# Float64 decode by masks on VectorE, block diagonals by a multiply, and a planner that knows partition turns: one fused attention, expert and mixing kernel on one core

## The chip, the cores and the metric

One core of a Trainium2 chip runs the whole program. The metric is device microseconds of one execution, from first to last instruction with a small fixed part around it. Engines are named as the profile names them: PE is TensorE (PEld its weight loads), DVE is VectorE, ACT is ScalarE, POOL is GpSimd, SP issues the DMAs. Each engine works through its own queue in order and waits on semaphores that the others raise.

## The reference, cut to what matters

Three stages follow one another for each of 8 batches of 576 tokens. In the reference's words, cut:

```python
k_p = k.reshape(B, H, 72, 8, D).mean(axis=3)          # pooled keys, 8 heads of 64
v_p = v.reshape(B, H, 72, 8, D).mean(axis=3)
x = softmax(q @ k_p.T / 8) @ v_p                      # attention, heads joined to 512
# 4 experts: causal attention with 64-wide heads, top 2 of 4 gates
out += gate_e * (softmax_causal(x @ wq[e], x @ wk[e]) @ (x @ wv[e]) @ wo[e])
theta = out @ w_theta
y = w_tok_r @ (out * cos(theta)) + w_tok_i @ (out * sin(theta))
u = out + y
result = u + maximum(u @ w_ch, 0)
```

Three of the weights, `w_theta`, `w_tok` and `w_ch`, come to the kernel as 64-bit floats. They have to be turned into pairs of 32-bit numbers (a rounded high part and the remainder) before PE can use them.

## The kernel before

Every product is made of three matmuls on a high and a low part (`mm3`), and the parts are made by ACT (a copy that rounds, the high part) and DVE or POOL (a subtraction, the low part). A first stage, up to about 500 us, runs attention and the experts for the 8 batches; a second stage mixes tokens and channels for the 8 batches.

The program is written as a list of operations, each with its engine, and a planner (`Plan`) issues them. `Plan.add` records an operation and its dependencies, `price` gives it an assumed cost, `arrange` gives it a due time from two tables (`PARTS` for the part of the program, `SHIFT` for engine and tile), and `issue` simulates the five queues and picks, one at a time, the operation that can start first, ties by due time. The result is a fixed order for each engine. So a change of costs or tables moves instructions everywhere, though none is added by it.

The parts that the change touches:

- `pool_kv` (L713 to L752): for each batch it sums groups of 8 keys and values by three `tensor_tensor` adds (on POOL; some on DVE for batch 0, by `FIRST_DVE`), tiles `kt1`, `vt1` and `vt2`. Two heads lie in the two halves of the 128 partitions and go to a block-diagonal operand: `kbd` by two ACT copies of 64 partitions each, `vbd` by two ACT copies and two subtractions of 64 partitions each. The other two blocks hold zeros that were written once at the start by POOL. The rest of the values goes to `vrh`, `vrl` (64 wide) and is spread by two multiplications with a mask `hm` to `vrb0` and `vrb1`.
- `attn_half` (L754): per tile of 128 queries, scores go to PSUM `s`, DVE takes the maximum `mx`, ACT takes the exponentials `pp`: eight activations with an accumulated sum, or, for tiles named in `WHOLE` (batch 0: tiles 1 to 4; later batches: tile 0), two DVE additions, one activation over all 576 columns and one DVE sum `l`. Then `pm` and `pq` are scaled, turned by PE (`t`) and split to `pa` and `pr`. The low part of `pr` lies in its upper 64 partitions.
- `decode` (L672): a task of 256 or 288 columns. DMA brings `d_raw`; ACT adds 768 to the high words as floats (`d_s`) and takes the sign; DVE shifts and joins the words in `d_raw`; ACT takes the absolute value; POOL multiplies `d_s`; ACT copies to `d_hi`; POOL subtracts to `d_lo`; two DMAs take the parts to DRAM (`thD`, `tokD`). 26 tasks run among the first stage, 8 more (`wch`, straight to `chs`) at the start of the second.
- `load` (L538): the DMAs `kraw`, `qraw`, `vraw`, `vrem` on SP's queue.

## Time and profile before

| what | value |
| --- | --- |
| median of 3 runs | 982.76 us (980.51 to 984.83) |
| the profiled execution, its time | 980.56 us |
| its span, first to last instruction | 978.8 us |
| PE busy | 916.0 us, 94% of the span |
| ACT busy | 650.3 us, 66% |
| DVE busy | 600.0 us, 61% |
| POOL busy | 516.7 us, 53% |
| mean granted TensorE clock | 0.992 of full speed |

Busy time is the time in which an engine had at least one instruction in flight. Instructions of one engine overlap at their ends, so sums of durations are above busy time. The profile gives stretches of the span (windows), groups of instructions by tile and shape (lines), what ended an engine's waits, the chain of work that ended last, and the instructions in order of time.

### The profile page before, as it was taken

To read this page: it belongs to the slowest core of one execution; us is meant where nothing else is said; L and a number is where in the kernel's file an instruction comes from. 1 tells how busy PE (TensorE), PEld (TensorE's weight loads), DVE (VectorE), ACT (ScalarE), POOL (GpSimd) and SP (SyncE) were. 2 spreads that over 40 slices of the span, in tenths; PEclk is the share of its full clock that TensorE was granted. 3 is DMA by queue.
4 is the path that set the end of the run, shared out by engine and by line. 5 is a ranking of instruction groups with operands and counts; after the bars stand their busy time and mean duration, and the time that the engine had idled before them with its cause. 6 is when DMAs were issued, how large, how long until landed. Compare 5 with 4: busy or idle time off the path is not lost.

```text
span 978.8 us, 19095 instructions
## 1 busy us (share of the span) xinstructions
PE 916.0 (94%) x6384; PEld 858.5 (88%) x6384; DVE 600.0 (61%) x1718; ACT 650.3 (66%) x2026; POOL 516.7 (53%) x693
## 2 busy tenths in 40 slices
PE   2888999999899999999888999999999999999998
PEld 2887988898889899988866799999999999999998
DVE  5877887787878788887756745272424534262412
ACT  4689989798888999987768864262535444363510
POOL 7877777577386755544355774261625335151420
PEclk9999999999999999999989999999999999999999
DMA  9444445335444433334277413020110202010001
GB/s 279 138 143 122 122 123 150 115 108 140 119 118 116 136 96 87 89 103 115 51 232 243 154 44 92 1 85 13 38 56 13 80 1 70 1 38 13 25 25 49
DMA packets 78434, 91.63 MB, mean 94 GB/s; under 512 B 11264, under 2 KB 60928, under 8 KB 78336
## 3 DMA queue, kind: packets, MB, share of 16 engines
q1 hardware_dynamic: 78336, 90.41, 31.4%
q8 instruction: 51, 0.84, 0.4%
q14 instruction: 47, 0.39, 0.1%
HBM read 58.34 MB, written 26.28 MB: 86 GB/s over the span
## 4 chain that ended last, share of the span: by engine, by line
PE 64%; ACT 17%; DVE 8%; DMA 4%; POOL 3%; issue 3%; SPq 1%; POOLq 0%; ACTq 0%; DVEq 0%
PE acc L466 46%; PE s L466 14%; PE t L466 4%; ACT pp L466 4%; ACT pt L466 2%; DMA kh<-kh 2%; ACT pev L466 2%; ACT qs L466 1%; DVE s L466 1%; ACT kh L466 1%; ACT pa L466 1%; DVE pa L466 1%; DMA qraw<-in_qT_dram 1%; ACT xT L466 1%; DVE kl L466 1%
## 5 line engine op out<-in xcount | busy, mean ns | idle before, releaser
L466 PE MATMUL acc<-toks,z 128*128 128x288 f32 x1536 | 242.3, 297 | 2.0 <-ACT z L466 1.0
L466 PEld LDWEIGHTS acc<-toks,z 128*128 128x128 f32 x1536 | 223.9, 188 | 9.5 <-POOL z L466 1.8
L466 POOL TENSOR_TENSOR us<-u,us 128x288 fp32r<-128x288 f32 x64 | 51.9, 811 | 198.4 <-ACT us L466 198.3
L466 PE MATMUL acc<-xT,wqs 128*128 128x256 f32 (+1 forms) x768 | 123.3, 303 | 3.4 <-DVE logit L466 1.4
L466 PE MATMUL acc<-us,chs 128*128 128x288 f32 x768 | 114.1, 297 | 0.6 <-DVE o L466 0.5
L466 PEld LDWEIGHTS acc<-xT,wqs 128*128 128x128 f32 x768 | 106.4, 189 | 7.5 <-PE acc L466 3.4
L466 PEld LDWEIGHTS acc<-us,chs 128*128 128x128 f32 x768 | 107.9, 188 | 5.0 <-DVE o L466 1.5
L466 DVE TENSOR_TENSOR u<-acc,xt 128x288 f32<-128x288 f32 x64 | 29.1, 455 | 132.4 <-PE acc L466 132.4
L466 ACT CAST us<-u 128x288 fp32r<-128x288 f32 x64 | 27.6, 431 | 120.6 <-DVE u L466 120.5
L466 POOL TENSOR_TENSOR z<-zf,z 128x512 fp32r<-128x512 f32 x64 | 81.9, 1298 | 33.7 <-ACT z L466 33.6
L466 POOL TENSOR_SCALAR pev<-pev,lb,G 128x128 f32<-128x128 f32 (+4 forms) x80 | 52.5, 657 | 72.6 <-DVE lb L466 30.0
L466 DVE TENSOR_TENSOR pt<-t,pt 128x512 fp32r<-128x512 f32 (+4 forms) x160 | 75.7, 484 | 15.2 <-ACT pt L466 13.2
L466 ACT ACTIVATE pp<-s,mx 128x72 f32<-128x72 f32 x232 | 74.6, 336 | 6.6 <-DVE mx L466 6.0
L466 PE MATMUL acc<-wvs,xT 128*128 128x260 f32 x480 | 77.6, 292 | 1.2 <-DVE kl L466 0.4
L466 DVE CUSTOM_DVE_ANT_0 s<-s,mask 128x128 f32<-128x128 f32 (+2 forms) x144 | 69.6, 494 | 14.7 <-PE s L466 12.7
L466 ACT CAST pt<-t 128x512 fp32r<-128x512 f32 (+4 forms) x160 | 67.8, 437 | 13.8 <-PE t L466 12.9
L466 PE MATMUL s<-kbd,qraw 128*128 128x144 f32 x320 | 60.3, 311 | 16.2 <-DMA qraw<-in_qT_dram 12.3
L466 PE MATMUL acc<-pt,v 128*128 128x320 f32 (+4 forms) x416 | 68.1, 296 | 5.6 <-ACT yg L466 1.6
L466 PE MATMUL s<-kh,qs 128*128 128x128 f32 (+2 forms) x192 | 62.3, 355 | 10.3 <-DMA kh<-kh 8.0
L466 PEld LDWEIGHTS acc<-pt,v 128*128 128x128 f32 x416 | 60.7, 191 | 11.2 <-ACT yg L466 3.1
L466 PEld LDWEIGHTS acc<-wvs,xT 128*128 128x128 f32 x480 | 65.5, 189 | 4.0 <-ACT yg L466 0.8
L466 PE MATMUL s<-wos,ys 128*128 128x512 f32 x192 | 66.1, 402 | 0.4 <-DVE zf L466 0.3
(177 smaller groups left out, 2244.8 us busy)
## 6 DMA issues: line engine op xcount, KB each, us to landing
qraw<-in_qT_dram SPq DMA_DIRECT2D x40, 256.0 KB, 3.6
out_dram<-o SPq DMA_DIRECT2D x64, 144.0 KB, 1.8
kraw<-in_kT_dram SPq DMA_DIRECT2D x15, 576.0 KB, 4.1
yraw<-ygD SPq DMA_DIRECT2D x16, 512.0 KB, 4.3
vraw<-in_vm_dram SPq DMA_DIRECT2D x15, 512.0 KB, 4.1
d_raw<-in_wtok_dram SPq DMA_DIRECT2D x18, 288.0 KB, 2.9
...
```

The lines of the kernel that those rows point to most:

```text
L466: o.ins = o.fn(*[a.real() if isinstance(a, View) else a for a in o.args], **{k: a.real() if isinstance(a, View) else a for k, a in o.kw.it ...
```

## The change

1. Decode. Two of ACT's passes (add and sign) become one DVE `tensor_scalar` that yields 0 or 1 for a word that is to be flushed; the absolute value becomes a mask in DVE's shift and one more DVE `scalar_tensor_tensor` that puts the sign and top bit back. ACT keeps the rounding copy, POOL its two operations. The pair goes to one tile `d_both` and by one DMA to DRAM.
2. Block diagonals. `kbd` and the doubled values are made by one multiplication with a column mask (`half`, `half64`) over 128 partitions, on POOL (DVE for some of batch 0); ACT rounds `vbd` by one copy and POOL subtracts once. All the sums share one tile `kv`. `vrh` and `vrl` become the two halves of one tile, with one multiplication by `hm`; `pq` is written twice so that `pr` has two whole tiles. Zero fills at the start go.
3. `WHOLE` for later batches is now tiles 0 and 2.
4. The planner adds 118 ns when an operation's first partitions differ from those of the one before on its engine (`TURN`), assumes a longer DMA (`DMA_LAT` 1700, and 1.7 times the bytes between on-chip tiles), and has new tables with a few parts of their own for the last batch of the first stage and the first of the second.

```diff
-WHOLE = {1, 2, 3, 4}, {0}
+WHOLE = {1, 2, 3, 4}, {0, 2}
-    "first": (-1302.83, 63.19), "kv first": (-249.24, 366.9), "attn first 0": (-2208.92, 30.55),
+    "first": (467.48, 10.11), "kv first": (72.08, 204.57), "attn first 0": (-1468.16, 177.1),
...
+        if eng == "DMA" and all(isinstance(a, View) and not a.root.pool.dram for a in args[:2]):
+            o.bytes *= 1.7
+    TURN = 118.0
+
-    DMA_ISSUE, DMA_LAT, DMA_RATE, DMA_ALL, DMA_SLOT, RELEASE = 600.0, 1300.0, 184.0, 262.0, 150.0, 130.0
+    DMA_ISSUE, DMA_LAT, DMA_RATE, DMA_ALL, DMA_SLOT, RELEASE = 600.0, 1700.0, 184.0, 262.0, 150.0, 130.0
...
-                t = free[e]
                 for o in cs:
+                    t = free[e] + (self.TURN if o.base != base[e] else 0.0)
...
-        A.activation(s, hi_w.bitcast(F32), AF.Copy, bias=FLUSH)
-        V.tensor_scalar(t, hi_w, 3, 0x40000000, op0=OP.logical_shift_left, op1=OP.bitwise_xor)
+        V.tensor_scalar(s, hi_w.bitcast(F32), FLUSH, FLUSH, op0=OP.add, op1=OP.not_equal)
+        V.tensor_scalar(t, hi_w, 3, 0x3FFFFFFF, op0=OP.logical_shift_left, op1=OP.bitwise_and)
         V.scalar_tensor_tensor(t, lo_w, 29, t, op0=OP.logical_shift_right, op1=OP.bitwise_or)
-        A.activation(s, s, AF.Sign, bias=flush)
-        A.activation(t.bitcast(F32), t.bitcast(F32), AF.Abs)
+        V.scalar_tensor_tensor(t, hi_w, -0x40000000, t, op0=OP.bitwise_and, op1=OP.bitwise_or)
         P.tensor_tensor(s, s, t.bitcast(F32), op=OP.mult)
         A.copy(hi, s)
         P.tensor_tensor(lo, s, f(hi), op=OP.subtract)
...
-        parts = decode(src, n, dec)
-        for d, p in zip(dst, parts):
-            D.dma_start(d, f(p))
+        D.dma_start(dst, f(decode(src, n, dec)))
...
-            for e in range(2):
-                s_ = slice(64 * e, 64 * e + 64)
-                A.activation(kbd[s_, p:p + n, e], t[s_, :, 0], AF.Copy, scale=1.0 / 64)
+            X.tensor_tensor(kbd[:, p:p + n], t[:, :, 0:1].to_broadcast([128, n, 2, 72]),
+                            half64[:, None, :, None].to_broadcast([128, n, 2, 72]), op=OP.mult)
...
-            for e in range(2):
-                s_ = slice(64 * e, 64 * e + 64)
-                A.copy(vbd[0][s_, p:p + n, e], t[s_, :, 0])
-                X.tensor_tensor(vbd[1][s_, p:p + n, e], t[s_, :, 0], f(vbd[0][s_, p:p + n, e]), op=OP.subtract)
+            X.tensor_tensor(t[:, :, 2:4], t[:, :, 0:1].to_broadcast([128, n, 2, 64]),
+                            half[:, None, :, None].to_broadcast([128, n, 2, 64]), op=OP.mult)
+            A.copy(vbd[0][:, p:p + n], t[:, :, 2:4])
+            X.tensor_tensor(vbd[1][:, p:p + n], t[:, :, 2:4], f(vbd[0][:, p:p + n]), op=OP.subtract)
...
-            X.tensor_tensor(pq[:, 0], pp[:, :, 64:72], l[:, :, None].to_broadcast([128, 8, 8]), op=OP.mult)
+            X.tensor_tensor(pq, pp[:, None, :, 64:72].to_broadcast([128, 2, 8, 8]),
+                            l[:, None, :, None].to_broadcast([128, 2, 8, 8]), op=OP.mult)
...
-            A.copy(pr[0:64, o:o + new], t1[:64, 0, n_])
-            V.tensor_tensor(pr[64:128, o:o + new], t1[:64, 0, n_], f(pr[0:64, o:o + new]), op=OP.subtract)
+            A.copy(pr[0][:, o:o + new], t1[:, 0, n_])
+            V.tensor_tensor(pr[1][:, o:o + new], t1[:, 0, n_], f(pr[0][:, o:o + new]), op=OP.subtract)
```

Three places in the issue order show it. First, SP's queue from the start of the program, before:

```order
L466 DMA vraw<-in_vm_dram 128x1024
L466 DMA kraw<-in_kT_dram 128x1152
L466 DMA pm<-in_vm_dram 128x512
L466 DMA vrem<-in_vr_dram 64x512
L466 DMA pev_161<-in_kT_dram 128x576
L466 DMA pev_164<-in_kT_dram 128x576
L466 DMA pm<-in_vm_dram 128x512
L466 DMA qraw<-in_qT_dram 128x4x128 x3
```

and now (`pev` holds keys here, `pm` values, `pod` a weight):

```order
L486 DMA kraw<-in_kT_dram 128x1152
L486 DMA pev_95<-in_kT_dram 128x576
L486 DMA pev_107<-in_kT_dram 128x576
L486 DMA vrem<-in_vr_dram 64x512
L486 DMA pm<-in_vm_dram 128x512 x2
L486 DMA qraw<-in_qT_dram 128x4x128
L486 DMA pod_177<-in_wvg_dram 128x260
L486 DMA vraw<-in_vm_dram 128x1024
```

The keys now come first, one query tile is asked for before the large `vraw`, and the other two query tiles come later.

Second, ACT's queue behind its first activation, before:

```order
L466 CAST vbd_95<-vt_175 64x2x64 x2
L466 ACTIVATE kbd<-kt_191 64x2x72 x2
L466 CAST vrh<-vt_205 64x64
L466 ACTIVATE kbd<-kt_213 64x72 x2
L466 CAST vrh<-vt_205 64x64
L466 ACTIVATE pp_150,suma_138<-s,mx 128x72 x4
```

and now:

```order
L486 CAST wvs_211<-pod_177 128x260
L486 ACTIVATE pp_157,suma_145<-s,mx 128x72 x8
L486 CAST wvs_211<-pod_183 128x260
L486 CAST vbd_249<-kv 128x256
L486 CAST wvs_211<-pev_95 128x260
```

ACT no longer stands between the sums and `kbd`; the eight exponentials of the first tile follow a weight's rounding directly.

Third, DVE's queue around the first 288-wide decode task, before:

```order
L466 RECIPROCAL l<-l 128x8
L466 TENSOR_SCALAR d_raw<-d_raw 128x288
L466 SCALAR_TENSOR_TENSOR qs_166<-acc,qs_166 64x320
L466 TENSOR_TENSOR pr<-t,pr 64x128
L466 TENSOR_TENSOR pa_3326<-t,pa_3317 128x4x128
```

and now (the task's two `scalar_tensor_tensor` follow some twenty rows on):

```order
L486 TENSOR_REDUCE m_1743<-gates_164 128x5
L486 TENSOR_SCALAR d_s<-d_raw 128x288
L486 TENSOR_REDUCE lb<-sum_132 128x2
L486 RECIPROCAL m_1743<-m_1743 128x5
L486 TENSOR_SCALAR d_t<-d_raw 128x288
L486 RECIPROCAL lb<-lb 128x2
```

DVE has two instructions of the first kind where it had one.

## Rows read from the trace of the kernel before

**Rows 1.** Windows: stretch; its length; PE, PEld, DVE, ACT, POOL busy; PEclk; DMA share; GB/s.

```profile
100.00:480.00 380.00, 359.17 (x2630) 336.04 (x2630) 306.01 (x1063) 336.06 (x1275) 235.82 (x373) 1.00 0.40 112
480.00:560.00 80.00, 69.55 (x388) 57.81 (x387) 53.82 (x123) 63.91 (x148) 45.20 (x44) 0.96 0.63 196
560.00:979.00 419.00, 415.19 (x2889) 398.13 (x2887) 167.48 (x292) 180.40 (x337) 158.95 (x144) 1.00 0.12 38
```

**Rows 2.** The page's chain that ended last, share of the span by engine.

```profile
PE 64%; ACT 17%; DVE 8%; DMA 4%; POOL 3%; issue 3%; SPq 1%; POOLq 0%; ACTq 0%; DVEq 0%
```

**Rows 3.** DVE's waits, 100 to 480 us: total us, times, longest us.

```profile
DVE xT L466 <- ACT xT L466: 8.7, 16, 2.5
...
DVE kl L466 <- ACT kh L466: 5.4, 8, 1.0
```

**Rows 4.** Groups on ACT by shape, 100 to 480 us: busy us, mean ns | idle before.

```profile
L466 ACT ACTIVATE pp<-s,mx 128x72 f32<-128x72 f32 x184 | 59.3, 338 | 2.3 <-DVE mx L466 1.9
...
L466 ACT ACTIVATE d_s<-d_s,flush 128x288 f32<-128x288 f32 x18 | 9.8, 546 | 0.2
L466 ACT ACTIVATE d_raw<-d_raw 128x288 f32<-128x288 f32 x18 | 8.6, 480 | 1.5 <-DVE d_raw L466 1.4
L466 ACT ACTIVATE d_s<-d_raw 128x288 f32<-128x288 f32 x18 | 8.6, 479 | 1.8 <-DMA d_raw<-in_wtok_dram 1.3 <-POOL d_lo L466 0.4
...
L466 ACT ACTIVATE kbd<-kt 64x144 f32<-64x144 f32 x20 | 6.5, 324 | 0.6 <-PE s L466 0.3
...
L466 ACT ACTIVATE pp<-pp 128x576 f32<-128x576 f32 x5 | 3.4, 684 | 2.1 <-DVE pp L466 2.1
```

**Rows 5.** ACT in order of time, from 14 us: start us, length us.

```profile
14.42 0.31 ACT L466 ACTIVATE pp<-s,mx 128x72 f32<-128x72 f32 x1
...
14.72 0.32 ACT L466 ACTIVATE pp<-s,mx 128x72 f32<-128x72 f32 x1
```

**Rows 6.** Groups on DVE by shape, 100 to 480 us, columns as in rows 4.

```profile
L466 DVE SCALAR_TENSOR_TENSOR d_raw<-d_raw 128x288 int32<-128x288 int32 x18 | 8.5, 472 | 0.3
...
L466 DVE TENSOR_SCALAR d_raw<-d_raw 128x288 int32<-128x288 int32 x18 | 5.7, 319 | 0.3 <-ACT d_s L466 0.2
...
L466 DVE TENSOR_TENSOR pp<-s,mx 128x288 f32<-128x288 f32 x10 | 4.4, 454 | 0.1
...
L466 DVE TENSOR_REDUCE l<-pp 128x8 f32<-128x584 f32 x5 | 3.8, 756 | 1.0 <-ACT pp L466 1.0
```

**Rows 7.** DVE in order of time, from 252 us, columns as in rows 5.

```profile
252.15 0.47 DVE L466 CUSTOM_DVE_ANT_0 s<-s,mask 128x256 f32<-128x256 f32 x1
...
252.53 0.48 DVE L466 TENSOR_TENSOR kl<-acc,kh 64x320 fp32r<-64x320 f32 x1
253.09 0.16 DVE L466 TENSOR_REDUCE lb<-sum 128x2 f32<-128x4 f32 x1
```

**Rows 8.** Groups on POOL by shape, 100 to 480 us, columns as in rows 4.

```profile
L466 POOL TENSOR_TENSOR pm<-pp,l 128x512 f32<-128x512 f32 x29 | 30.7, 1058 | 24.0 <-ACT pev L466 5.4 <-DVE l L466 5.2 <-ACT d_raw L466 3.9
...
L466 POOL TENSOR_TENSOR kt<-kt 128x288 f32<-128x288 f32 x9 | 7.3, 811 | 0.1
```

**Rows 9.** All engines in order of time, first 20 us: start, length, idle before and its releaser.

```profile
12.28 1.78 PE L466 MATMUL s<-kbd,qraw 128*128 128x144 f32 x6 [12.28 <-DMA qraw<-in_qT_dram]
...
16.46 0.53 ACT L466 ACTIVATE kbd<-kt 64x72 f32<-64x72 f32 x2
...
17.05 2.77 PE L466 MATMUL s<-kbd,qraw 128*128 128x144 f32 x10 [2.99 <-ACT kbd L466]
```

**Rows 10.** Instructions of tile d_raw over the whole span: min/median/max ns.

```profile
L466 DVE TENSOR_SCALAR d_raw<-d_raw x34: 254/310/2429, 43.2 to 588.4; 128x288 int32<-128x288 int32 x18, 128x256 int32<-128x256 int32 x16
```

**Rows 11.** POOL and DVE in order of time, from 588 us, columns as in rows 5.

```profile
588.22 2.41 POOL L466 TENSOR_TENSOR ys<-yraw,ys 128x1024 fp32r<-128x1024 f32 x1
588.35 2.43 DVE L466 TENSOR_SCALAR d_raw<-d_raw 128x256 int32<-128x256 int32 x1
```

**Rows 12.** PE's waits, 100 to 480 us, columns as in rows 3.

```profile
PE s L466 <- DMA kh<-kh: 5.6, 6, 2.1
```

193 lines of the change are left out of this document (100 added, 93 removed), and 7 rows, old and new, of the table PARTS.

## The prediction, made before the changed kernel was run

> **What bounds the kernel now.** I read the windows first. From 560 us on PE is busy 415.2 of 419 us [rows 1]: the second stage is PE's own work, and the change adds and removes no matmul (6,226 PE rows in the issue order of both). So a gain must come from the first stage or from the passage between the two. From 100 to 480 us PE is busy 359.2 of 380, ACT 336.1 (88%), DVE 306.0 (81%), POOL 235.8 (62%) [rows 1]. PE's named waits there are small; the largest is 5.6 us for the DMA that moves `kh` between partition halves [rows 12]. But a busy PE hides short gaps, since matmuls overlap. The chain of waits says more: 64% of the span is PE, 17% ACT, 8% DVE [rows 2]. The second stage alone (419 of 978.8 us, nearly all PE) is 43% of the span, so in the first stage some 21% of the span is PE against 17% ACT: there, ACT is on the chain almost as much as PE. And DVE waits mostly for ACT: six rows of that kind, from 8.7 us for `xT` down to 5.4 for `kl`, sum to 40.7 us [rows 3]. So ACT's queue is what paces DVE, and through it PE, between 100 and 480 us.
>
> **Decode, on ACT.** Three ACT passes of a 288-wide task go: 479 + 546 + 480 ns = 1.5 us [rows 4]. Instructions of one engine overlap by about 0.1 us (a DVE one of 0.47 us is followed after 0.38 us [rows 7]), so I count 1.2 us. Of the 26 tasks in the first stage 24 lie between 100 and 480 us, 18 of them 288 wide; the six of 256 are priced alike: 29 us.
>
> **Decode, on DVE.** One `tensor_scalar` (319 ns) and one `scalar_tensor_tensor` (472 ns) come on top [rows 6], less 0.18 us of overlap: 24 x 0.61 = 15 us. One DMA in place of two takes an issue off SP for each task, which no chain shows; I count nothing. If the DVE steps were covered fully, this part would cost nothing; uncovered, 15 us.
>
> **`WHOLE`.** One tile more for each later batch, seven in all, some six of them in this stretch. Eight exponentials at 0.30 us from start to start [rows 5] become one of 684 ns, 0.58 after overlap [rows 4]: 6 x 1.8 = 11 us off ACT. DVE gets two additions of 454 ns and a sum of 756 in place of a small one that I take at the 0.16 of another small sum [rows 6, 7]: 6 x 1.4 = 8.5 us.
>
> **Block diagonals.** ACT loses the 20 `kbd` copies (324 ns, 0.22 after overlap [rows 4]) for 4.5 us, and half of its `vbd` and `vrh` copies, which I price like `kbd` at 2.5 us. POOL gets a product of 288 columns for each pair of `kbd` and of `vbd` blocks, priced at the 811 ns of an addition of that width, and loses one of two spreads of `vr`, priced like a 512-wide product at 1058 [rows 8]: 4 x 0.81 - 1.06 = some 2 us for a batch, 14 in all, beside 144 us in which POOL is idle [rows 1]. I cost it at nothing; that cover is gone only if POOL's chain for `kbd` is late when the scores start, and then it costs at most those 2 us a batch, 14 in all. One tile `kv` in place of three puts the sums of keys and values one behind the other; they run far ahead of their use, also nothing, same bound.
>
> **Turns.** In the issue orders, neighbours on an engine whose operands start at different partitions fall from 344 to 267 on DVE and from 278 to 170 on ACT. A 64-partition `kl` of 0.48 us is followed only after 0.56 us, where an instruction of 128 is followed 0.09 us before its end [rows 7]. At 0.1 us each DVE gets some 7 us back here. ACT's turns I leave out of its sum, as the trace shows no price for them: nothing to 10 us.
>
> **The sum for 100 to 480 us.** ACT loses 29 + 11 + 4.5 + 2.5 = 47 us: from 88% to 76%. DVE gains 15 + 8.5 - 7 = 16.5 us: from 81% to 85%. What DVE waits for ACT lies between the whole 40.7 us and nothing. If waiting behind a busy engine goes with busy over idle share, it falls from 0.88/0.12 to 0.76/0.24, to 43%: 23.5 us come back, an estimate from rows 1 and 3 that I take because ACT stays a busy engine. Then 16.5 - 23.5 = -7 us, with ends of +16.5 (no wait shrinks) and -24 (all do). What is late next is DVE itself.
>
> **The start.** PE's second group of scores waits 2.99 us for a `kbd` copy that stands behind exponentials on ACT [rows 9]; POOL now makes that block itself. The first matmul waits until 12.28 us for a query tile [rows 9]. Some 2,560 KB were asked for up to that tile, 512 KB (`vraw`) fewer now: between nothing and a fifth of 12.28, 2.5 us; I take 1.5. Two query tiles now stand behind `vraw` and the next batch's keys, which may give some of it back. I take -4 us, between nothing and -5.5.
>
> **The passage and the rest.** From 480 to 560 us ACT is busy 63.9 of 80 and PE's granted clock is 0.96 [rows 1]: lighter decode work gives perhaps 1 us, between -4 and +3, as the order there is new. The wait for `kh` (5.6 us) may move either way with the longer DMA that the planner assumes; I count nothing, between -5.6 and +5. In the second stage eight decode tasks move to DVE, which is busy 167 of 419 us [rows 1]: nothing, at most 2.4 us for one held instruction (below).
>
> **Sum.** The profiled execution took 980.56 us (span 978.8 and 1.76 around it): 980.56 - 7 - 4 - 1 = 968.6. The median of the runs is 2.2 above that execution, so on its scale 971 us.
>
> **The rivals.** *Slower: DVE stands behind POOL.* A decode `tensor_scalar` began at 588.35 us, 0.13 us after POOL's `ys` subtraction, and ended with it: 2.43 us [rows 11], against a minimum of 254 ns [rows 10]. So a DVE instruction with operands on chip can be held for a whole POOL instruction. The change adds 48 such DVE instructions between 100 and 480 us, where a POOL product takes about 1 us [rows 8]. If each is held 0.4 us, a bit under half of that, DVE gets 19 us more: 980.56 + 2.2 - 12 + 19 = 990. It turns slower than now from 0.25 us each, and by over 0.5% from 0.35. Against it: the mean there is 319 ns [rows 6], so holds cost 0.07 us so far.
>
> The Trainium skill (SBUF — State Buffer, "Who interferes with whom") states that a DVE instruction with two on-chip inputs, or one in a two-port mode, and a GpSimd instruction that reads shut each other out for the whole instruction. By that rule all the added decode steps are open to such holds, which is the rival above; the trace agrees at 588 us, and not for the mean.
>
> *No change: PE's order is what counts.* PE is already busy 359 of 380 us [rows 1]; if ACT's share of the chain passes to DVE and POOL as ACT empties, only part of the start is left: 980.56 + 2.2 - 3 = 980. For it: DVE at 85% would be as tight as ACT was. Against it: most of DVE's waits have ACT's name.
>
> *Far faster.* All of DVE's waits for ACT go (-24), the start gives 4 and the passage 1, and the `kh` waits vanish (-5.6): 980.56 + 2.2 - 34.6 = 948. It wants ACT never to be late, at 76%: unlikely.
>
> That the change does not do what it says is ruled out for the counts, which the order shows.
>
> **Chances.** Forecast 971: 0.52. Far faster: 0.13. No change: 0.21. Slower: 0.14. A measurement of this kernel tells about 0.5%, 4.9 us, from no change. Faster by more: 0.52 + 0.13 = 0.65; within: 0.21; slower: 0.14. The range of 8 in 10 goes from 953, short of the far case, to 987, which takes in no change and leaves out the slower case.
>
> **What would show it.** Right: ACT busy some 50 us less in the first stage, DVE some 15 more, DVE's waits for ACT near 17 us in a stretch of this length, the wait for `kbd` at the start gone, the second stage starting 10 us or so earlier and lasting as long. Wrong: `d_s` or `d_t` steps on DVE with means over 0.6 us (the slower rival); or ACT's idle time growing by the whole 47 us with no step of PE's coming earlier (no change). The forecast is most at risk in how much of DVE's waiting ACT's relief gives back, for no row of this trace prices that.

## The result: 1.3% slower, most of it lost in the first 115 us

The changed kernel takes 994.35 us (median of 4 runs, 991.10 to 997.76) beside 981.63 us for the kernel before (4 runs on the same chip). The ratio is 1.0127, with a 95% interval of 1.0080 to 1.0174. The forecast was 971 us. The profiled execution took 995.76 us, span 994.0, against 980.56 and 978.8: the two traces lie 15.2 us apart, the medians 12.7.

The windows of the changed kernel (stretch; its length; PE, PEld, DVE, ACT, POOL busy; PEclk; DMA share; GB/s), to be read beside [rows 1]:

```profile
100.00:480.00 380.00, 358.59 (x2614) 338.80 (x2613) 319.47 (x1092) 290.36 (x1077) 247.35 (x372) 0.98 0.39 111
480.00:560.00 80.00, 69.65 (x408) 59.05 (x406) 52.98 (x143) 61.51 (x153) 42.78 (x47) 0.98 0.62 189
560.00:994.00 434.00, 425.93 (x2954) 407.68 (x2952) 177.23 (x324) 182.95 (x335) 162.51 (x151) 1.00 0.12 39
```

From 100 to 480 us ACT is busy 45.7 us less than before and DVE 13.5 us more, near the 47 and 16.5 of the prediction. DVE's figure is in part luck: only 20 decode tasks reach DVE in this stretch (24 before), as six in place of two come ahead of it. PE is busy as long as it was. The chain that ended last, by engine, beside [rows 2]:

```profile
PE 67%; DVE 10%; ACT 8%; POOL 6%; DMA 5%; issue 3%; SPq 1%; ACTq 0%; POOLq 0%; DVEq 0%
```

ACT's share of the chain fell from 17% to 8%, and nothing was won by it. The longest of DVE's waits from 100 to 480 us (total us, times, longest us), beside [rows 3], and two of ACT's in the same stretch (L466 is the kernel before, L486 the changed one):

```profile
DVE pt L466 <- ACT pt L466: 6.7, 16, 1.1
...
ACT pt L466 <- PE t L466: 6.9, 9, 2.0
...
ACT v L466 <- PE acc L466: 3.3, 4, 0.9
...
DVE pt L486 <- ACT pt L486: 11.1, 17, 1.2
DVE s L486 <- PE s L486: 8.9, 21, 1.7
DVE xT L486 <- ACT xT L486: 6.6, 12, 1.1
...
ACT pt L486 <- PE t L486: 11.8, 20, 1.5
ACT v L486 <- PE acc L486: 10.3, 17, 1.0
```

DVE still waits for ACT's copy of a PE result, and ACT in turn waits for that result: what ACT gave up became ACT's idle time. ACT's named waits for PE in this stretch sum to 20.0 us before and 47.4 now.

**Where the time went.** The two traces are best laid over each other by PE's work. I price each matmul at one duration for its operands and shape (the lower quartile of the distance to the next one in the kernel before) and ask when a given amount of this work is done; the total is 815.9 us. Below, "late" always means this difference to the trace of the kernel before, and a "mark" an amount of work done.

| work done, us | 10 | 30 | 40 | 50 | 60 | 100 | 200 | 300 | 360 | 420 | 800 |
|---|---|---|---|---|---|---|---|---|---|---|---|
| before, at | 34.7 | 59.7 | 73.3 | 91.6 | 102.4 | 151.2 | 280.2 | 401.3 | 478.3 | 563.3 | 959.0 |
| changed, at | 43.3 | 66.5 | 78.6 | 102.8 | 114.6 | 166.9 | 294.5 | 418.8 | 490.4 | 576.4 | 974.1 |
| late by | 8.6 | 6.8 | 5.3 | 11.2 | 12.3 | 15.6 | 14.3 | 17.5 | 12.2 | 13.2 | 15.0 |

The changed kernel is 8.6 us late at the first mark, wins 3 back up to 40 us of work, and loses 6 between 40 and 50; with 60 us of work done it is 12.3 us late. From there to the end of the first stage it swings up to 17.5 and comes back (12.2 at 360); the passage costs 1 us, and the second stage 2. So the steady stretch, on which the forecast rested, came out even, and the start lost, in two places.

**What stands at the start.** PE in order of time in the changed kernel (start us, length us, then the idle time before and what ended it), beside [rows 9]:

```profile
10.55 2.26 PE L486 MATMUL s<-kbd,qraw 128*128 128x144 f32 x8 [10.55 <-DMA qraw<-in_qT_dram]
14.88 2.29 PE L486 MATMUL s<-kbd,qraw 128*128 128x144 f32 x8 [2.07 <-DMA qraw<-in_qT_dram]
...
37.77 0.80 PE L486 MATMUL acc<-pr,vrb 128*128 128x256 f32 x2 [7.87 <-DVE vrb L486]
38.36 0.84 PE L486 MATMUL acc<-pa,vbd 128*128 128x256 f32 x3
```

The gains that the prediction saw are there: the first scores come 1.7 us earlier, and the wait for `kbd` is gone, though 2.07 us for the second query tile stand in its place. But then PE stands still for 7.87 us, for `vrb`. DVE in order of time, before and now:

```profile
12.03 1.05 DVE L466 TENSOR_TENSOR vrb<-vrh,hm 128x512 fp32r<-128x512 f32 x1 [0.32 <-ACT vrh L466]
...
33.63 0.41 DVE L486 TENSOR_TENSOR kv<-vrem 64x256 f32<-64x256 f32 x1
...
36.35 0.63 DVE L486 TENSOR_TENSOR vr<-kv,vr 64x64 fp32r<-64x64 f32 x1
37.02 0.69 DVE L486 TENSOR_TENSOR vrb<-vr,hm 128x512 fp32r<-128x512 f32 x1
```

Before, the sums over the remaining values had a tile of their own (`vt2`) and the first `vrb` stood at 12.0 us. Now all sums share the one tile `kv`, the remainder is its last user for batch 0, and DVE takes up its chain at 33.6 us.

In this wait PE's granted clock falls, and it is still low when matmuls run again. Windows, columns as above, first one of the kernel before, then the changed one:

```profile
35.00:40.00 5.00, 3.92 (x33) 3.67 (x32) 4.08 (x14) 3.67 (x11) 4.94 (x8) 1.00 0.25 71
...
30.00:35.00 5.00, 0.00 (x0) 0.00 (x0) 4.98 (x15) 1.02 (x2) 2.85 (x4) 0.90 0.46 133
35.00:40.00 5.00, 2.23 (x9) 2.07 (x10) 3.07 (x7) 1.65 (x5) 3.96 (x3) 0.50 0.49 161
...
80.00:85.00 5.00, 2.42 (x12) 2.21 (x13) 4.23 (x16) 4.60 (x22) 4.57 (x6) 0.68 0.47 136
85.00:90.00 5.00, 5.00 (x29) 5.00 (x29) 1.96 (x7) 2.18 (x10) 4.84 (x8) 0.64 0.38 103
100.00:105.00 5.00, 4.47 (x21) 4.15 (x20) 2.38 (x11) 3.40 (x15) 1.61 (x3) 0.50 0.08 24
```

0.50 is the lower of the two levels, 1.2 of 2.4 GHz; a value between is a stretch with both. Three matmuls `acc<-pa,vbd` take 0.84 us from 38.36 us on; in the kernel before the same three, at the full clock, take 0.51:

```profile
29.24 0.51 PE L466 MATMUL acc<-pa,vbd 128*128 128x256 f32 x3
```

Over the whole span, 1 less the mean granted clock, times the span, is 17.9 us in the changed kernel (0.982, 994.0) and 7.8 us before (0.992, 978.8). A wait of PE is so paid for a second time where matmuls follow it at the lower clock. The second loss, between 78.6 and 102.8 us, has both parts: PE's waits there sum to 7.5 us (3.5 in the same work before), and the clock is low in part of it.

Beside the tile, the new order changed one thing more at the start: six decode tasks begin in the first 100 us (their `d_s` at 19.6, 31.0, 40.4, 48.0, 62.7 and 78.3 us), three before (on ACT, at 19.6, 54.3 and 87.9 us). Each brings work to DVE, POOL, ACT and SP's queue.

### The profile page after: what moved, and what is told of

Read it like the earlier page. It is cut to its first block, busy times and chain, and to the rows that moved or that the text cites. A ratio compares the mean times of both kernels' runs of the same rounds, so it can differ in the third digit from the quotient of the medians.

```text
span 994.0 us, 18769 instructions
## 1 busy us (share of the span) xinstructions
PE 919.3 (92%) x6384; PEld 865.8 (87%) x6384; DVE 626.6 (63%) x1806; ACT 589.1 (59%) x1760; POOL 525.8 (53%) x688
## 4 chain that ended last, share of the span: by engine, by line
PE 67%; DVE 10%; ACT 8%; POOL 6%; DMA 5%; issue 3%; SPq 1%; ACTq 0%; POOLq 0%; DVEq 0%
PE acc L486 49%; PE s L486 13%; PE t L486 5%; POOL z L486 2%; DVE s L486 2%; DVE mx L486 1%; DVE pt L486 1%; ACT pp L486 1%; ACT pev L486 1%; DMA qraw<-in_qT_dram 1%; DVE pa L486 1%; DMA kh<-kh 1%; DVE kl L486 1%; DVE qs L486 1%; SPq L486 1%
## 5 line engine op out<-in xcount | busy, mean ns | idle before, releaser
L486 PE MATMUL acc<-toks,z 128*128 128x288 f32 x1536 | 232.3, 297 | 0.8 <-POOL z L486 0.8
L486 PEld LDWEIGHTS acc<-toks,z 128*128 128x128 f32 x1536 | 217.1, 188 | 5.1 <-POOL z L486 1.2
L486 POOL TENSOR_TENSOR us<-u,us 128x288 fp32r<-128x288 f32 x64 | 51.8, 810 | 211.6 <-ACT us L486 211.6
L486 PE MATMUL acc<-xT,wqs 128*128 128x256 f32 (+1 forms) x768 | 124.5, 306 | 2.1 <-DVE kl L486 1.0
L486 DVE TENSOR_TENSOR u<-acc,xt 128x288 f32<-128x288 f32 x64 | 29.2, 456 | 151.9 <-PE acc L486 151.9
L486 PE MATMUL acc<-us,chs 128*128 128x288 f32 x768 | 111.0, 297 | 1.9 <-POOL us L486 1.7
L486 PEld LDWEIGHTS acc<-xT,wqs 128*128 128x128 f32 x768 | 108.0, 193 | 4.8 <-DVE qs L486 1.3
L486 PEld LDWEIGHTS acc<-us,chs 128*128 128x128 f32 x768 | 106.3, 188 | 6.3 <-POOL us L486 3.5
L486 POOL TENSOR_TENSOR z<-zf,z 128x512 fp32r<-128x512 f32 x64 | 81.9, 1300 | 32.4 <-ACT z L486 32.2
L486 ACT CAST us<-u 128x288 fp32r<-128x288 f32 x64 | 27.5, 430 | 109.4 <-DVE u L486 109.0
L486 DVE TENSOR_TENSOR pt<-t,pt 128x512 fp32r<-128x512 f32 (+4 forms) x160 | 75.0, 486 | 17.6 <-ACT pt L486 15.2
L486 DVE CUSTOM_DVE_ANT_0 s<-s,mask 128x128 f32<-128x128 f32 (+2 forms) x144 | 69.2, 497 | 15.8 <-PE s L486 14.9
L486 ACT CAST pt<-t 128x512 fp32r<-128x512 f32 (+4 forms) x160 | 66.6, 430 | 21.1 <-PE t L486 19.9
L486 POOL TENSOR_SCALAR pev<-pev,lb,G 128x128 f32<-128x128 f32 (+4 forms) x80 | 52.7, 661 | 49.3 <-DVE lb L486 17.5
L486 PE MATMUL s<-kbd,qraw 128*128 128x144 f32 x320 | 60.9, 317 | 17.3 <-DMA qraw<-in_qT_dram 12.6
L486 PE MATMUL acc<-pt,v 128*128 128x320 f32 (+4 forms) x416 | 67.1, 300 | 8.0 <-DVE qs L486 3.7
L486 PEld LDWEIGHTS acc<-pt,v 128*128 128x128 f32 x416 | 62.0, 196 | 14.0 <-DVE qs L486 4.8
L486 PE MATMUL acc<-wvs,xT 128*128 128x260 f32 x480 | 70.4, 289 | 0.1
L486 PEld LDWEIGHTS s<-kbd,qraw 128*128 128x128 f32 x320 | 49.2, 209 | 20.4 <-issue 10.5
L486 ACT CAST z<-zf 128x512 fp32r<-128x512 f32 x64 | 38.8, 621 | 46.7 <-DVE zf L486 26.2
L486 PEld LDWEIGHTS acc<-wvs,xT 128*128 128x128 f32 x480 | 62.8, 189 | 0.9 <-DVE xT L486 0.3
L486 PE MATMUL s<-kh,qs 128*128 128x128 f32 (+2 forms) x192 | 61.0, 349 | 0.9 <-DMA kh<-kh 0.5
```

The lines of the kernel that those rows point to most:

```text
L486: o.ins = o.fn(*[a.real() if isinstance(a, View) else a for a in o.args], **{k: a.real() if isinstance(a, View) else a for k, a in o.kw.it ...
```

## Experiments with a new plan: they measure the new order

All times are medians; ratios are to the kernel before on the same chip, with 95% intervals. The first four kernels change one thing and let the planner order everything anew. The lateness below is against the kernel before on the scale of the table above.

**The remainder's own tile.**

```diff
-t = awork.tile([128, 2, 4, 72], F32, name="kv", bufs=1)[:64, 0, :, :64]
+t = awork.tile([64, 4, 64], F32, name="kv2", bufs=1)
```

> The changed kernel, but the sums of the values' rest (vrem) get a tile of their own; all else of the change stays, and the planner orders anew: vrb moves from row 83 to row 39 of DVE's queue. Theory A (one tile kv for all sums makes batch 0's vrb late; that is the loss at the start): PE's wait of 7.9 us for vrb goes, and the kernel takes about 994 - 8 = 986 us. Theory B (DVE is overloaded by the decode that now runs on it during the first 130 us, and vrb is only where it shows): DVE's backlog shows in another wait, under 3 us come back, over 991. Theory C (the new tables and costs of the planner give a worse order everywhere): under 3 us come back as well, and the gain at the start is lost again by 500 us.

Measured: 1033.50 us, ratio 1.0554 [1.0519, 1.0589]. The wait for `vrb` goes, and when 60 us of work are done the kernel is only 2.0 us late (changed kernel 12.3). But it is 9.7 us late at 100, 34.8 at 400 and 51.7 at the end. With the tile apart and a new order around it the early loss goes; the total tells of that other order behind it.

**Decode held back** until the first projections of batch 0, by a dependency of each decode's transfer on the last matmul of that part.

```diff
-D.dma_start(raw[:, :n], src)
+o = D.dma_start(raw[:, :n], src)
+if hold:
+    o.deps.add(hold[0])
+    hold[0].users.append(o)
```

> The changed kernel, but in the plan no decode task may start before the last projection matmul of batch 0; the decode itself stays on DVE. Theory B: the second part of the loss (from +5 us at 73 us of the span to +14 at 140, PE waiting for pa, qs and pt from DVE) goes, some 5 to 8 us: 986 to 989. Theory A: vrb stays late (row 78 of DVE's queue), PE's wait for it stays near 8 us, and the time is within 3 us of 994. Theory C: within 3 us of 994 too.

Measured: 1014.17 us, 1.0366 [1.0337, 1.0395]. Late by 6.2 us at 10, 18.0 at 60, 33 at the end. The first decode begins at 92.8 us here, so the load of decode is not what makes this start late; but the order is a new one.

**The old decode in the changed kernel.**

```diff
-V.tensor_scalar(s, hi_w.bitcast(F32), FLUSH, FLUSH, op0=OP.add, op1=OP.not_equal)
+A.activation(s, hi_w.bitcast(F32), AF.Copy, bias=FLUSH)
...
-V.scalar_tensor_tensor(t, hi_w, -0x40000000, t, op0=OP.bitwise_and, op1=OP.bitwise_or)
+A.activation(s, s, AF.Sign, bias=flush)
+A.activation(t.bitcast(F32), t.bitcast(F32), AF.Abs)
```

> The changed kernel with the decode of before (sign and absolute value on ACT, two DMAs); tile kv, WHOLE, planner and tables stay as changed. Theory B: DVE is relieved of two instructions for each of 26 tasks, some 20 us, and 5 to 10 us come back: 984 to 989. Theory A: vrb is as late as it was (row 82), within 3 us of 994. If the masks on DVE do bring what the change wanted of them, this is slower than the changed kernel, over 997.

Measured: 1050.37 us, 1.0727 [1.0700, 1.0754], late by 68.6 us at the end.

**One sum tile in the kernel before,** with the due times of the old names:

```diff
-t = awork.tile([64, 4, 64], F32, name="vt2", bufs=1)
+t = awork.tile([128, 2, 4, 72], F32, name="kv", bufs=1, kind="vt")[:64, 0, :, :64]
```

(and the same for `kt1` and `vt1`).

> The kernel before, with nothing changed but that its three sum tiles are one (due times kept): in DVE's queue the first vrb moves from row 37 to row 71. Theory A: PE waits for vrb at the start and the kernel takes 5 to 9 us more than before, 987 to 991. Theories B and C: within 3 us of 982.

Measured: 1020.72 us, 1.0428 [1.0397, 1.0459]. PE's waits from 10 to 80 us:

```profile
PE acc L468 <- DVE vrb L468: 12.6, 1, 12.6
```

So with the shared tile the wait for `vrb` comes in the other kernel too, and PE is 15.8 us late at the first mark. The lesson of the four is one of method. The first three are 20 to 56 us slower than the changed kernel that they edit, the fourth 42 us slower than the kernel before: whatever is edited, the kernel loses once the planner runs again. Most likely its tables suit one list of operations; no run has new costs or tables with the old operations. Such totals say nothing about the edit. From here on the order is frozen: the planner's list for the kernel that is edited is computed, and single operations are exchanged in it where they stand. The diffs show these exchanges as plain code; in the kernels the new form is attached to the operation whose place it takes.

## Experiments with the order kept: what each part costs

**In the kernel before,** one part at a time.

Decode by masks:

```diff
-A.activation(s, hi_w.bitcast(F32), AF.Copy, bias=FLUSH)
+V.tensor_scalar(s, hi_w.bitcast(F32), FLUSH, FLUSH, op0=OP.add, op1=OP.not_equal)
...
-A.activation(s, s, AF.Sign, bias=flush)
-A.activation(t.bitcast(F32), t.bitcast(F32), AF.Abs)
+V.scalar_tensor_tensor(t, hi_w, -0x40000000, t, op0=OP.bitwise_and, op1=OP.bitwise_or)
```

> The kernel before with its order kept; only the decode is changed, each step in the place of an old one: ScalarE's first step becomes VectorE's comparison, its Sign goes, its Abs becomes VectorE's merge of the top bits. ScalarE loses three instructions of 480 to 546 ns in each of 42 decodes (about 63 us in all), VectorE gains two, 0.8 to 1.1 us (34 to 46 us in all, 26 of the 42 before the passage). Theory A (relief of ScalarE and load of VectorE about cancel; the loss is one of order): 972 to 982 us. Rival B (VectorE's added work costs by itself): 986 to 996 us. The prediction's own reckoning (ScalarE's relief comes back): about 971 us.

Measured: 986.13 us (10 runs), 1.0070 [1.0047, 1.0093]. It costs 7 us. No mark up to 100 us of work is late by over 1 us, and the lateness grows slowly through the first stage; the trace shows only half of the cost, 3.6 us at 800, as its run is the fastest of the ten (984.34).

Block diagonals by a mask:

```diff
-for e in range(2):
-    A.activation(kbd[s_, p:p + n, e], t[s_, :, 0], AF.Copy, scale=1.0 / 64)
+X.tensor_tensor(kbd[:, p:p + n], t[:, :, 0:1].to_broadcast([128, n, 2, 72]),
+                half64[:, None, :, None].to_broadcast([128, n, 2, 72]), op=OP.mult)
```

(`vbd` likewise: a product, a copy and a subtraction for two copies and two subtractions).

> The kernel before with its order kept; only the block diagonals of kbd and vbd are changed, each step in the place of an old one: two ScalarE copies with scale become one product with a mask, two copies and two subtractions become one product, one copy and one subtraction. The remainder's chain stays as it was, and so do the three sum tiles. Theory A: within 4 us of the kernel before, 975 to 983 us, since ScalarE's 2.99 us wait at the start may go. Rival B (POOL's longer products hold the next batch's scores): 984 to 992 us.

Measured: 990.56 us, 1.0103 [1.0063, 1.0142]. The curve is 0.9 us late at 10, 5.1 at 20 and 7.9 at 40 us of work, 8.2 at 280 and 9.3 at the end. Nearly all of it falls between 35 and 80 us of the run, where one DVE instruction stands out:

```profile
39.48 3.79 DVE L474 TENSOR_TENSOR wqs<-pev,wqs 128x512 fp32r<-128x512 f32 x1
```

In the kernel before the same subtraction takes 0.69 us:

```profile
38.80 0.69 DVE L466 TENSOR_TENSOR wqs<-pev,wqs 128x512 fp32r<-128x512 f32 x1
```

PE waits 2.4 us for its result. In the changed kernel's own start no DVE instruction is held like this; its two `wqs` subtractions take 0.68 us each.

Whole rows in the tile 2 of later batches (eight exponentials become two additions, one exponential and one sum):

```diff
-WHOLE = {1, 2, 3, 4}, {0}
+WHOLE = {1, 2, 3, 4}, {0, 2}
```

> The kernel before with its order kept and only the tile 2 of batches 1 to 7 by whole rows: in each, eight ScalarE instructions of 338 ns with as many reads of sums become two VectorE subtractions (454 ns), one ScalarE instruction (684 ns) and VectorE's sum over the row in place of a short one (756 ns). ScalarE loses about 2 to 3 us in each of seven tiles, VectorE gains about 1.5 us. All three edits in place took +24 us, mask decode +7 and block diagonals +12 of it; if the costs add, this one gives +3 to +8 us: 982 to 987 us. If ScalarE's relief counts, 974 to 978 us.

Measured: 979.88 us (12 runs), 0.9991 [0.9971, 1.0012]. It costs nothing.

All three in place (the diffs above together):

> The kernel before with its order kept and all three edits in place: the decode by masks, the block diagonals of kbd and vbd by a mask, and the whole-row softmax for the tile 2 of the later batches (eight ScalarE instructions with sums become two VectorE subtractions, one ScalarE instruction and one VectorE sum over the row). It differs from the changed kernel by the order, the three sum tiles and the remainder's chain. Theory A (the edits are worth a little, the order loses it): 970 to 981 us, so the order alone is worth +13 to +24 us in the changed kernel. Rival B (the edits cost by themselves): 988 to 1000 us, and the order is no more than a part of it.

Measured: 1003.41 us, 1.0255 [1.0196, 1.0313]. That is 24 us, where the three alone make 18; its four runs spread from 1000.9 to 1011.5, so the difference is hardly clear of noise. So the parts do cost in this order, against my theory at that point that only a new order loses; the changed kernel, some 10 us faster than this with its own order, wins part of it back.

**Whole rows, and the mask from batch 1 on:**

```diff
+WHOLE = {1, 2, 3, 4}, {0, 2}
...
+if b > 0:
+    X.tensor_tensor(kbd[:, p:p + n], t[:, :, 0:1].to_broadcast([128, n, 2, 72]),
+                    half64[:, None, :, None].to_broadcast([128, n, 2, 72]), op=OP.mult)
```

> The kernel before with its order kept, whole rows in the tile 2 of batches 1 to 7 (which alone gave 979.88 us), and the block diagonals by the mask in batches 1 to 7 only; batch 0 keeps its copies, and the decode is the old one. Theory F (the mask costs only where the start waits for GpSimd and VectorE; later the products hide): 975 to 981 us. Rival (GpSimd's longer products are felt in every batch): 984 to 992 us.

Measured: 990.30 us, 1.0116 [1.0095, 1.0136]. The rival's number, but not its reason. The curve is even at 10 us of work (-0.3), 3.9 us late at 20, 7.0 at 40, 8.9 at 200 and 9.1 at the end, so it is not felt in every batch. What is left at the start is batch 1's first product. POOL and DVE of this run around it:

```profile
37.94 0.31 POOL L474 TENSOR_TENSOR vt<-vt 64x64 f32<-64x64 f32 x1
38.22 0.66 POOL L474 TENSOR_TENSOR kbd<-kt,half 128x288 f32<-128x288 f32 x1
38.85 0.29 POOL L474 TENSOR_TENSOR pq<-pp,l 128x64 f32<-128x64 f32 x1
39.10 1.04 POOL L474 TENSOR_TENSOR pm<-pp,l 128x512 f32<-128x512 f32 x1
40.11 1.38 POOL L474 TENSOR_TENSOR kt<-kraw 128x576 f32<-128x576 f32 x1
41.57 1.70 POOL L474 TENSOR_TENSOR kt<-kt 128x288 f32<-128x288 f32 x2
...
38.51 3.54 DVE L474 TENSOR_TENSOR wqs<-pev,wqs 128x512 fp32r<-128x512 f32 x1
```

The subtraction begins while POOL's new product runs and ends at 42.05 us, 0.5 us behind the first gap in POOL's queue, at 41.5 us. In the kernel before ACT makes `kbd`, and the same subtraction, begun at 38.80 us, gets in between two of POOL's instructions:

```profile
38.25 0.31 POOL L466 TENSOR_TENSOR vt<-vt 64x64 f32<-64x64 f32 x1
38.63 0.30 POOL L466 TENSOR_TENSOR pq<-pp,l 128x64 f32<-128x64 f32 x1
38.89 1.52 POOL L466 TENSOR_TENSOR pm<-pp,l 128x512 f32<-128x512 f32 x1
```

Here it is POOL's `pm` that stretches, to 1.52 us from the 1.04 of the other run. Why DVE gets in there and not in the run above, no row shows. The Trainium skill (SBUF — State Buffer, "Who interferes with whom") says that two such instructions shut each other out for a whole instruction and that the one issued first wins; the trace agrees that one is held and the other not, but DVE was held through four of POOL's instructions, not one.

**ACT's relief and DVE's load by themselves,** again in the kernel before. ACT's three decode steps left out:

```diff
-A.activation(s, hi_w.bitcast(F32), AF.Copy, bias=FLUSH)
-A.activation(s, s, AF.Sign, bias=flush)
-A.activation(t.bitcast(F32), t.bitcast(F32), AF.Abs)
-P.tensor_tensor(s, s, t.bitcast(F32), op=OP.mult)
+P.tensor_tensor(s, t.bitcast(F32), t.bitcast(F32), op=OP.mult)
```

> The kernel before with its order kept, and ScalarE's three decode steps (the copy with 768 added, Sign, Abs) left out of all 42 decodes; nothing is put on VectorE; GpSimd multiplies the same tile with itself, so the decoded weights are wrong. ScalarE loses about 1.5 us for each decode, 63 us in all, some 32 us of them between 100 and 480 us. The prediction held that half of what ScalarE gives up there comes back, which is 16 us: 962 to 966 us. Theory C (ScalarE is not the engine that the rest waits for; what waits for it waits for PE's results that it copies, so its freed time becomes idle time): 975 to 980 us.

Measured: 974.10 us, 0.9929 [0.9909, 0.9949]. (There are 34 decodes, 26 in the first stage and 8 in the second; the expectations here and below count 42, and sums of durations where busy time is the fairer measure.) ACT's busy time over the span falls from 650.3 to 612.2 us, by 38, and 6.7 us come back, about a sixth. The window from 100 to 480 us:

```profile
100.00:480.00 380.00, 358.36 (x2645) 336.02 (x2643) 307.52 (x1071) 312.08 (x1211) 232.84 (x373) 1.00 0.40 113
```

and the longest of DVE's waits for ACT in it:

```profile
DVE xT L474 <- ACT xT L474: 8.8, 15, 2.5
DVE l L474 <- ACT pp L474: 7.8, 11, 2.8
DVE v L474 <- ACT v L474: 6.9, 12, 1.1
DVE pt L474 <- ACT pt L474: 6.0, 15, 1.1
```

ACT's share falls from 88% to 82%. By the prediction's rule the six waits of DVE for ACT should fall to (0.82/0.18)/(0.88/0.12) = 62% of their 40.7 us, to 25; they are 38.4. So these waits are for the most part no queue behind ACT's other work: DVE waits for a copy that ACT itself can make only when PE is done. The other side agrees: ACT's named waits for PE in this stretch rise from 20.0 to 37.2 us.

DVE's added steps put beside the old ones:

```diff
 A.activation(s, hi_w.bitcast(F32), AF.Copy, bias=FLUSH)
+V.tensor_scalar(d_t.bitcast(F32), hi_w.bitcast(F32), FLUSH, FLUSH, op0=OP.add, op1=OP.not_equal)
...
 A.activation(t.bitcast(F32), t.bitcast(F32), AF.Abs)
+V.scalar_tensor_tensor(d_t, lo_w, -0x40000000, d_t, op0=OP.bitwise_and, op1=OP.bitwise_or)
```

> The kernel before with its order kept and ScalarE's decode as it was; behind the old first step VectorE does the new comparison as well, behind the old Abs a merge of the same form as the new one, both into a tile that nobody reads. VectorE gains 0.8 to 1.1 us for each of 42 decodes, 34 to 46 us in all, 22 to 28 of them before the passage. Theory C (VectorE is the engine on which PE waits, ScalarE's relief gives nothing): 984 to 992 us, as much as or more than the mask decode in place took (986.13). Rival (VectorE's load is hidden too, and the mask decode's +7 us came from its longer chain through two engines): 977 to 982 us.

Measured: 990.84 us, 1.0097 [1.0076, 1.0119]. DVE's busy time grows by 27 us over the span (600.0 to 627.1) and in the window from 100 to 480 us from 306.0 to 318.2. PE's work is 1.7 us late at 50, 5.5 at 200, 9.3 at 360 and 11.0 at the end. So in this order a microsecond of DVE costs about twice what one of ACT gives (10/27 against 6.7/38); the two make +3.3 us of the +7 that both together took, and the rest is not accounted for.

**In the changed kernel,** whose own order is kept in the same way.

The old decode put back in place (the diff of the third run, now with the order kept):

> The changed kernel with its own order kept and the old decode back, each step in the place of a new one: VectorE's comparison becomes ScalarE's first step, VectorE's merge becomes ScalarE's Sign and Abs. VectorE loses 0.8 to 1.1 us in each of 42 decodes, ScalarE gains 1.5 us. Theory C by the two runs that had each by itself (VectorE's steps 10 us, ScalarE's steps 7 us): about 3 us less, 989 to 993 us. If the new order is fitted to the new decode, the exchange costs in this direction too: 995 to 1003 us.

Measured: 1006.78 us, 1.0269 [1.0246, 1.0291].

The old copies for `kbd` and `vbd` put back in place:

```diff
-X.tensor_tensor(kbd[:, p:p + n], t[:, :, 0:1].to_broadcast([128, n, 2, 72]),
-                half64[:, None, :, None].to_broadcast([128, n, 2, 72]), op=OP.mult)
+for e in range(2):
+    A.activation(kbd[s_, p:p + n, e], t[s_, :, 0], AF.Copy, scale=1.0 / 64)
```

> The changed kernel with its own order kept and the block diagonals of kbd and vbd made by copies again: one product becomes two ScalarE copies with scale; a product, a copy and a subtraction become two copies and two subtractions. The remainder's chain and the shared tile kv stay. If the mask costs at the start in this order too, as it did in the order of before (+12 us there, all of it in the first 40 us): 984 to 990 us. If the early loss is one of the queues' order and not of the products: 993 to 1000 us.

Measured: 1001.82 us, 1.0226 [1.0203, 1.0249].

DVE's two added decode steps left out:

```diff
-V.tensor_scalar(s, hi_w.bitcast(F32), FLUSH, FLUSH, op0=OP.add, op1=OP.not_equal)
-V.scalar_tensor_tensor(t, hi_w, -0x40000000, t, op0=OP.bitwise_and, op1=OP.bitwise_or)
-P.tensor_tensor(s, s, t.bitcast(F32), op=OP.mult)
+P.tensor_tensor(s, t.bitcast(F32), t.bitcast(F32), op=OP.mult)
```

> The changed kernel with its own order kept and VectorE's two added decode steps, the comparison and the merge of the top bits, left out of all 42 decodes (GpSimd multiplies the same tile with itself; the decoded weights are wrong). VectorE loses 34 to 46 us in all. Theory C (VectorE's microseconds count about a quarter, as in the order of before, where they cost 10 us): 983 to 987 us. If the new order hides them: 992 to 996 us.

Measured: 994.91 us, 1.0150 [1.0127, 1.0173], the changed kernel's time. The window from 100 to 480 us:

```profile
100.00:480.00 380.00, 357.99 (x2615) 338.09 (x2614) 305.08 (x1055) 290.44 (x1074) 244.36 (x373) 0.98 0.39 111
```

and PE's longest wait from 20 to 130 us:

```profile
PE acc L494 <- DVE vrb L494: 8.1, 1, 8.1
```

Here DVE is at 305 us of 380, as little as before, and ACT at 290, and PE comes at most 2 us earlier on the way and 0.3 at 800 us of work. The expectation of a quarter of DVE's time fell: in the changed kernel's order its added work is hidden. An exchange in either direction costs in the order made for the other form, so the price of a part holds for one order only. What the changed kernel loses is then not the load of DVE's two added steps.

## Experiments on the changed kernel's start

**`vrb` early.** Batch 0's chain for the remainder is put behind DVE's last `kbd` product, with sums of its own; all else stays where it was.

```diff
+early = [o for o in order if o.tag == "vr"]
+order = [o for o in order if o.tag != "vr"]
+at = max(i for i, o in enumerate(order) if o.kind == "DVE.kbd") + 1
+order[at:at] = early
```

> The changed kernel with the planner's order kept, word for word, but for eight instructions: batch 0's chain for the values' remainder (three sums, ScalarE's copy, the subtraction, the product vrb) is put right behind VectorE's last product for kbd, and its sums lie in a tile of their own. Theory A (the loss begins with the shared tile kv, whose last user in the ring is this chain): PE's wait of 7.9 us for vrb goes, the curve of PE's work is 7 to 9 us ahead of the changed kernel's from 40 us on, and the time is 984 to 988 us. Rival B (the order behind it is fitted to the late chain, or VectorE is the bound): the wait goes, but the lead is used up by 130 us and the time is 992 to 996 us.

Measured: 996.78 us, 1.0157 [1.0098, 1.0217]. `vrb` is ready at 11.1 us, and PE stands still as long as before. Its longest wait behind the first query tile, from 0 to 110 us:

```profile
PE acc L498 <- DVE xT L498: 7.8, 1, 7.8
```

ACT in order of time:

```profile
36.59 0.62 ACT L498 CAST wqs<-pev 128x512 fp32r<-128x512 f32 x1 [2.09 <-DMA pev<-in_wqk_dram]
37.11 0.65 ACT L498 ACTIVATE xT<-acc 128x256 fp32r<-128x256 f32 x2
```

PE's next product has to wait until `xT` has emptied its PSUM buffer. ACT could do that at 30 us, but its queue has the rounding of the last weight first, and that weight's transfer goes late, since its staging tile `pev` is held by a DVE subtraction at 32.4 us. My theory A, that the late chain by itself loses 8 us, fell: the chain for `vrb` and this one were late by about the same.

**The weight's chain and `xT` mended, decode moved.** On top of the early `vrb`, the subtraction, the transfer and ACT's rounding of that weight come earlier, two `xT` go ahead of the fourth `pp`, and the decodes 1 to 5 come 9 to 12 us later.

```diff
+move(find("DVE.wvs", w)[1], find("DVE.pm", "attn first 0")[0])
+move(dma[3], dma[2])
+move(acts[3], acts[2])
...
+for k in (0, 1):
+    move(xa[k], pp[3], True)
...
+late = {1: 9.0, 2: 12.0, 3: 12.0, 4: 12.0, 5: 12.0, 6: 11.0, 7: 10.0, 8: 9.0, 9: 8.0, 10: 7.0, 11: 6.0, 12: 5.0, 13: 4.0, 14: 3.0, 15: 2.0, 16: 1.0}
```

> The changed kernel with the remainder's chain early (as in the run before) and, in the first 60 us, the queues mended where the trace of that run shows who is late: VectorE's low part of the fourth values' weight goes right behind its first pm, so that the tile pev is free, the last weight's transfer goes right behind the third's, ScalarE's copy of it behind the third's, the first two xT go ahead of the fourth pp on both engines, and the decodes 1 to 5 come 9 to 12 us later (shrinking to nothing by decode 17). Theory D (a chain through pev, SyncE's queue and ScalarE's queue, not vrb alone, holds PE at 30 us): PE's wait of 7.8 us for xT shrinks to under 2.5 us, PE's work at 40 us is 4 to 7 us ahead of the changed kernel's, and if nothing behind it is late for another reason the time is 986 to 990 us. Rival (what comes between 73 and 130 us does not care when it starts): 993 to 997 us.

Measured: 1013.28 us, 1.0325 [1.0301, 1.0350]. At 10 us of work the lateness is 5.2 us in place of 8.6, but it is 14.1 at 70 and 34 at the end. The next run, without the moved decodes, is 16 us faster, so moving them seems to cost more than the start could give; the run settles nothing.

**The same without moving the decode,** all four `xT` ahead of the second decode's copy and of the last weights' subtractions:

```diff
-late = {1: 9.0, 2: 12.0, 3: 12.0, 4: 12.0, 5: 12.0, 6: 11.0, 7: 10.0, 8: 9.0, 9: 8.0, 10: 7.0, 11: 6.0, 12: 5.0, 13: 4.0, 14: 3.0, 15: 2.0, 16: 1.0}
+late = {}
...
+for k in (2, 3):
+    move(xd[k], [o for o in q["DVE"] if o.kind == "DVE.wqs"][0], True)
+    move(xa[k], [o for o in q["ACT"] if o.kind == "ACT.d_both"][1], True)
```

> The changed kernel with the remainder's chain early and the queues of the first 40 us mended, and the decode left where it is: VectorE's low part of the fourth values' weight right behind its first pm, the last weight's transfer right behind the third's and ScalarE's copy of it behind the third's, ScalarE's four xT ahead of the second decode's copy (two of them ahead of the fourth pp too), VectorE's four xT ahead of the low parts of the last weights. Theory D: PE's wait of 7.8 us for xT falls under 3 us, the curve of PE's work is 4 to 8 us ahead of the changed kernel's at 40 us, and the lead is kept to the end: 986 to 991 us. Rival (the stretch from 73 to 130 us takes the lead back): 993 to 998 us.

Measured: 997.67 us, 1.0166 [1.0141, 1.0192]. PE is late by 2.5 us at 10 us of work, 6.1 us ahead of the changed kernel, as theory D wanted; at 20 it is late by 8.3 again. PE and POOL in order of time:

```profile
41.25 0.63 PE L585 MATMUL t<-ident,pm 128*128 128x128 f32 x4 [2.33 <-POOL kv L585]
...
38.91 1.45 POOL L585 TENSOR_TENSOR kv<-kraw 128x576 f32<-128x576 f32 x1
40.44 1.55 POOL L585 TENSOR_TENSOR kv<-kv 128x288 f32<-128x288 f32 x2
```

PE now waits while POOL sums the next batch's keys, and the granted clock falls to 0.56 in the 5 us from 45 us on.

**POOL's sums early as well.**

```diff
+for o in reversed([o for o in q["POOL"] if o.tag == "k1"]):
+    move(o, find("POOL.wvs", w)[0])
```

> The run h2 with one thing more: GpSimd's three sums over the first half of batch 1's keys (1.43 + 0.98 + 0.48 us) stand behind its first wvs at 15 us, where GpSimd was idle, in a tile of their own, and no longer ahead of the last pm of batch 0 at 39 us. Theory D: PE's waits of 2.33 us for pm and 0.86 us for kbd at 41 us go, the lead over the changed kernel at 20 to 30 us of PE's work is 3 to 6 us in place of h2's 0 to -2, and the time is 989 to 994 us. Rival E (every engine's queue in this stretch is late by about the same, so each mended wait uncovers the next): within 3 us of h2, 994 to 1000 us.

Measured: 994.21 us, 1.0144 [1.0116, 1.0172]. PE is late by 3.7, 6.8 and 5.8 us at 10, 20 and 30 us of work, less than the changed kernel (8.6, 7.9, 6.8), and by 15.3 at the end. PE's waits for POOL's sums are gone; in their place, from 20 to 130 us:

```profile
PE t L587 <- DVE pa L587: 4.7, 3, 2.1
PE t L587 <- DVE pm L587: 3.7, 1, 3.7
```

Rival E fits these runs: in the first 50 us ACT, DVE, POOL and SP's queue are late by about the same, and each mended wait uncovers the next. What brought that lateness into the new order, its tables and costs or the decode tasks that come earlier, no run shows: none has fewer early decodes with the order otherwise kept, or the old operations with the new tables. The second loss, the 6 us between 40 and 50 us of work, stays open as well; the four runs with a mended start have it too (5 to 7 us). There PE waits 2.5 us for DVE's `qs` in one piece and runs at a lower clock behind it (0.64 from 85 to 90 us), but no run moved that alone.

None of these kernels is clearly faster than the kernel before, but for the one that leaves ACT's decode steps out.

## Why the prediction was wrong, step by step

- *The start, -4 us: this step failed.* It came out at +12.3 (lateness at 60 us of work). The two gains named were there, but I followed PE's queue only to its second group of scores. The first product of values stood a little further down with its `vrb`, and I had costed the one tile `kv` at nothing ("they run far ahead of their use"). For batch 0 nothing runs ahead. The same tile in the kernel before, with a new plan, made the same wait (12.6 us). It is still not the whole cause: with `vrb` early in the changed kernel's order the total stays (996.78), as other queues are as late. Of the 12.3 us, some 6 fall in a second place, whose cause stays open.
- *100 to 480 us, -7 us: the mechanism failed, and the time came out at 0.* ACT lost 45.7 us for 47 forecast, DVE gained 13.5 for 16.5. But that "waiting behind a busy engine goes with busy over idle share" is false here: with ACT at 82%, DVE's six waits were 38.4 us and not 25, and 38 us off ACT gave 6.7 us and not half. In the changed kernel the six largest waits for ACT sum to 31.9 us, not 17. That DVE's 13.5 us cost next to nothing either is shown by the run without its steps: this order hides them. What the turns gave, 7 us in the forecast, no run has by itself.
- *Decode's price.* The first new step takes a mean of 586 ns where I took 319. The group of DVE from 100 to 480 us, and one of its rows with POOL's beside it:

```profile
L486 DVE TENSOR_SCALAR d_s<-d_raw 128x288 f32<-128x288 f32 x18 | 10.5, 586 | 0.7 <-DMA d_raw<-in_wtok_dram 0.6
...
196.70 1.41 POOL L486 TENSOR_TENSOR kv<-kraw 128x576 f32<-128x576 f32 x1
...
196.71 1.56 DVE L486 TENSOR_SCALAR d_s<-d_raw 128x288 f32<-128x288 f32 x1
```

  That is 4.8 us more in all, and hidden too. The mean hides two kinds: 14 of the 18 take 0.30 to 0.39 us, and four take 1.56 to 1.57, each begun 0.01 to 0.03 us after a POOL sum of 1.4 us and ended 0.2 us behind its end.
- *Block diagonals at nothing: right in place, wrong at the edge.* The bound of 2 us a batch was never used in the steady stretch; with the order of before, the start alone lost 7.9 us by 40 us of work, 4 of them at one DVE instruction held behind POOL.
- *`WHOLE`: taken as -11 + 8.5; alone it is 0 (0.9991).*
- *Passage -1 and second stage 0:* +1 and +2. *`kh`:* its waits, 5.6 us before, fell out of PE's longest rows, and nothing was won by that either.
- *The rivals.* The time is near that of the slower rival (990), but not by its mechanism: of the added decode steps from 100 to 480 us only four `d_s` were held for a whole POOL instruction, the `scalar_tensor_tensor` steps took 484 ns (472 before), and leaving the added steps out gives nothing. "No change: PE's order is what counts" had the steady stretch right; it too had a start that gains. The sign that the text named for it, ACT's idle time growing by the whole relief with no step of PE's earlier, is what the trace shows.
